# Attention with a threshold and two dense layers: k and q of a head pair turned by one crossbar transpose

## The chip, the cores and the metric

The kernel runs on one core of a Trainium2 chip. A core has five engines, each with its own instruction queue that is worked off in order: PE (TensorE, matrix products), DVE (VectorE), ACT (ScalarE), POOL (GpSimd) and SP (SyncE, which here only issues transfers). Sixteen DMA engines move data and can turn it on the way (the crossbar). The metric is device time of one execution in microseconds (us), lower is better.

## The reference

q, k and v have 8 batches, 8 heads, 576 rows and a head dimension of 64, in float32.

```
scores = matmul(q, k.T) / sqrt(64)
thresh = max(scores, axis=-1) - tau            # tau = 0.02
scores = where(scores >= thresh, scores, -1e9)
attn   = softmax(scores)
x      = matmul(attn, v)       # heads side by side: 4608 rows x 512
h      = x @ w_in              # 512 x 2048
out    = (h - tanh(h)) @ w_out # 2048 x 512
```

## The kernel before

**Pairs and slots.** Two heads of a batch make a pair; there are 32 (counted from 0). A pair has 1152 rows of q, nine tiles of 128: four of each head and one that the heads share. So there are 288 tiles, and the kernel is written out by hand as slots, one for each tile, 8 slots ahead for the scores: in slot s the scores of tile s + 8 are issued, the kink (threshold as a steep Prelu on ACT) of tile s + 5, the exponentials of tile s, and the product with v of tile s - 2. The two dense layers of an earlier batch lie between them, a few matmuls in a slot. Nothing is reordered: each engine gets its instructions in the order in which the slots issue them. The first scores of pair p come in slot 9p - 8, called `first` in the code.

**Why k and q are turned.** PE contracts over partitions, so k and q must lie with head dimension down the partitions. For accuracy each is also split into a high and a low half in float16 (`split`, lines 225 to 235, three POOL operations for each of k and q): 64 high and 64 low numbers fill 128 partitions. The split tile `khl` or `qhl` is 128 x 9 x 128, nine blocks of 128 x 128. Turning the blocks gives `kT` and `qT`, 128 x 1152. Scores need high and low parts crossed too, so POOL also copies kT with its halves exchanged to `kS` (`swap`, line 332, two copies).

**Two ways of turning.** For pairs 0 to 8 the blocks are turned on PE and copied from PSUM. From pair 9, the tenth, on (`k_by_dma`, `q_by_dma`), `turn` (line 311) issues a crossbar transpose of nine blocks from SP's queue, line 315, one for k and one for q. The tiles' threshold values z are turned the same way from pair 6 on: one transpose zT<-z of nine blocks for two tiles, issued on SP at line 454 as soon as the second tile's kink is issued; line 483 exponentiates zT on ACT five slots later. SP works all of these off in order, together with the stores of the output (line 620).

**When a step is issued.** For each pair from 8 on, a table gives the step and how many slots ahead of `first` it is issued: `LATER[0]` for even pairs, `LATER[1]` for odd ones, `FIRST_LATER` for pairs 8 and 9. In a step's name the first letter is the tensor, the second the step: 0, 1, 2 loads (issued on ACT's queue, in parts), s split on POOL, t turn, w swap on POOL. The table at lines 760 to 783 sets only the order in the queues; each step also waits for its data. An engine that waits holds all that is queued behind it.

**Buffers.** Raw k, q and v have two buffers each, split tiles two each, kT, qT and kS three each.

Of the kernel before, what the change touches and what calls it, by code (L numbers as in the profile page):

```python
# [11 lines left out]
FP16 = mybir.dt.float16  # L12
# [6 lines left out]
def kernel(  # L19
# [11 lines left out]
    nc = tc.nc  # L31
    P = 128

    B, H, S, D = q.shape
# [17 lines left out]
    TPP = 9  # L52
# [8 lines left out]
    W = 2 * S  # L61
# [51 lines left out]
    hl_pool = pool("hl", 2)  # L113
    qk_pool = pool("qk", 3)
# [29 lines left out]
    def load_part(p, t, part):  # L144


        b, h0 = p // HPAIR, 2 * (p % HPAIR)
        if part == 0:
            both = raw_pool.tile([P, AT_ONCE, 10, D], F32, name=f"{t}raw", tag=t)
            boths[t] = both  # L150
            for a in range(AT_ONCE):
                raws[p + a, t] = both[:, a, :, :]
        both = boths[t]
        rows = {"k": k, "q": q, "v": v}[t][b, h0 : h0 + 2 * AT_ONCE, :, :]
        heads = both.rearrange("p a (h c) d -> p (a h) (c d)", h=2)
        if t == "k":
            dst = both[:, :, 0:TPP, :].rearrange("p a c d -> p a (c d)")
            rows = rows.rearrange("(a h) s d -> a (h s) d", h=2).rearrange(
                "a (p c) d -> p a (c d)", c=TPP
            )  # L160
        elif t == "v":
            rows = rows.rearrange("h (p c) d -> p h (c d)", c=TPP)

            at, c0, c1 = V_PARTS[part]
            dst = heads[at : at + 64, :, c0 % 4 * D : (c1 - c0 + c0 % 4) * D]
            if c0 == 8:
                dst = heads[at : at + 64, :, 4 * D : 5 * D]
            rows = rows[:, :, c0 * D : c1 * D]
        elif part == 0:
            dst = heads[:, :, 0 : 4 * D]  # L170
            rows = rows[:, 0:512, :].rearrange("h (p c) d -> p h (c d)", c=4)
        else:
            dst = both[:, part - 1, 4, :]
            rows = rows[2 * part - 2 : 2 * part, 512:S, :].rearrange("h s d -> s h d")
        LOADER.dma_start(out=dst, in_=rows)
# [44 lines left out]
    for n in range(11):  # L220
        nc.tensor.matmul(out=pz, lhsT=zero[:, 0:P], rhs=zero, start=True, stop=True)

    hls = {}

    def split(p, t):
        x = raws.pop((p, t))[:, 0:9, :]
        hl = hl_pool.tile([P, TPP, 2, D], FP16, name=f"{t}hl", tag=t)
        nc.gpsimd.tensor_scalar(  # L228
            out=x, in0=x, scalar1=QKSC, scalar2=1.0, op0=ALU.mult, op1=ALU.mult
        )  # L230
        nc.gpsimd.tensor_copy(out=hl[:, :, 0, :], in_=x)
        nc.gpsimd.tensor_tensor(  # L232
            out=hl[:, :, 1, :], in0=x, in1=hl[:, :, 0, :], op=ALU.subtract
        )
        hls[p, t] = hl

    def split_first(t, part):
        cs = (slice(0, 5), slice(5, TPP))[part]
        r = raws[0, t][:, cs, :]
        if part == 0:  # L240
            hls[0, t] = hl_pool.tile([P, TPP, 2, D], FP16, name=f"{t}hl", tag=t)
        hl = hls[0, t][:, cs, :, :]
        if part == 0:
            nc.scalar.mul(out=hl[:, :, 0, :], in_=r, mul=QKSC)
            nc.vector.scalar_tensor_tensor(
                out=hl[:, :, 1, :], in0=r, scalar=QKSC, in1=hl[:, :, 0, :],
                op0=ALU.mult, op1=ALU.subtract,
            )
        else:
            nc.gpsimd.tensor_scalar(  # L250
                out=r, in0=r, scalar1=QKSC, scalar2=1.0, op0=ALU.mult, op1=ALU.mult
            )
            nc.gpsimd.tensor_copy(out=hl[:, :, 0, :], in_=r)
            nc.gpsimd.tensor_tensor(
                out=hl[:, :, 1, :], in0=r, in1=hl[:, :, 0, :], op=ALU.subtract
            )
# [13 lines left out]
    mats = {}  # L270


    def qk_tile(t):
        m = qk_pool.tile([P, W], FP16, name="kS" if t == "ks" else f"{t}T", tag=t)
        return m

    by_head = lambda ap: ap.rearrange("p (s h) -> p h s", h=2)
    in_heads = lambda ap: ap.rearrange("p (h s) -> p h s", h=2)
# [1 line left out]
    def turn_chunk(out, c, lhsT, mixed=True):  # L280
        rhs = ident_f16
        if c == 4 and mixed:
            out, rhs = in_heads(out), by_head(rhs)
        nc.tensor.matmul(
            out=out, lhsT=lhsT, rhs=rhs, is_transpose=True, start=True, stop=True
        )
# [17 lines left out]
    def q_by_dma(p):  # L304

        return p > DUAL

    def k_by_dma(p):
        return p > DUAL

    def turn(p, t):
        hl = hls.pop((p, t))
        if (q_by_dma if t == "q" else k_by_dma)(p):
            m = mats[p, t] = qk_tile(t)
            nc.sync.dma_start_transpose(
                out=m[:, 0:W].rearrange("p (c r) -> p c r", c=TPP),
                in_=hl.rearrange("p c a d -> p (c a d)"),
            )
            return
        ps = ps_big.tile([P, W], FP16, name=f"ps_{t}", tag="big")  # L320
        for c in range(TPP):
            turn_chunk(
                ps[:, c * P : (c + 1) * P], c, hl[:, c, :, :].rearrange("p a d -> p (a d)"),
                t == "q" or p < DUAL,
            )
        m = qk_tile(t)
        nc.vector.tensor_copy(out=m[:, 0:W], in_=ps)
        mats[p, t] = m
        if t == "k":
            swap(p)  # L330

    def swap(p):
        m = mats[p, "k"]
        sw = qk_tile("ks")
        for lo, hi in ((0, D), (D, 0)):
            o, i = sw[lo : lo + D, 0:W], m[hi : hi + D, 0:W]
            nc.gpsimd.tensor_copy(out=o, in_=i)  # L337
        mats[p, "ks"] = sw

    def turn_first(t, part):  # L340

        hl = hls[0, t[0]]
        c0, c1 = ((0, 5), (5, TPP))[part]
        pl, tag = (ps_y, "y") if t == "ks" else (ps_h, "h")
        ps = pl.tile([P, 5 * P], FP16, name=f"ps1_{t}", tag=tag)
        for c in range(c0, c1):
            o = ps[:, (c - c0) * P : (c - c0 + 1) * P]
            if t == "ks":
                for a in range(2):
                    turn_chunk(o[64 * a : 64 * a + 64, :], c, hl[:, c, 1 - a, :])  # L350
            else:
                turn_chunk(o, c, hl[:, c, :, :].rearrange("p a d -> p (a d)"))
        if part == 0:
            mats[0, t] = qk_tile(t)
        dst, n = mats[0, t][:, c0 * P : c1 * P], (c1 - c0) * P
        if part == 1 or t == "q":
            nc.scalar.copy(out=dst, in_=ps[:, 0:n])
        else:
            nc.vector.tensor_copy(out=dst, in_=ps[:, 0:n])
# [373 lines left out]
    def w_load(piece):  # L733
# [6 lines left out]
        else:  # L740
# [18 lines left out]

    LATER = {  # L760
        0: (
            ("kt", 11), ("qt", 7), ("k0", 18), ("q0", 17), ("v0", 13),
            ("q1", 14), ("v1", 10), ("ks", 12), ("qs", 8), ("vs", 4),
            ("kw", 6),
        ),
        1: (
            ("kt", 10), ("qt", 6), ("k0", 18), ("q0", 14), ("v0", 15),
            ("q1", 13), ("v1", 12), ("ks", 11), ("qs", 8), ("vs", 6),
            ("kw", 5),
        ),  # L770
    }
    FIRST_LATER = {
# [1 line left out]
            ("k0", 18), ("q0", 15), ("v0", 14), ("kt", 7), ("q1", 15),  # L774
            ("ks", 8), ("v1", 12), ("vs", 6), ("qs", 10), ("qt", 5),
            ("kw", 3),
        ),
        9: (
            ("kt", 10), ("qt", 6), ("k0", 18), ("q0", 14), ("v0", 15),
            ("q1", 13), ("v1", 12), ("ks", 11), ("qs", 8), ("vs", 6),  # L780
            ("kw", 5),
        ),
    }
    for p in range(DUAL, NPAIR):
        first = TPP * p - AHEAD
        at = lambda d, f: plan.setdefault(first - d, []).append(f)
        for what, d in FIRST_LATER.get(p) or LATER[p % 2]:
            t, w = what
            f = {
                "0": lambda p=p, t=t: load_part(p, t, 0),  # L790
                "1": lambda p=p, t=t: load_part(p, t, 1),
                "2": lambda p=p, t=t: load_part(p, t, 2),
                "s": lambda p=p, t=t: split_v(p) if t == "v" else split(p, t),
                "t": lambda p=p, t=t: turn(p, t),
                "w": lambda p=p, t=t: swap(p) if k_by_dma(p) else None,
            }[w]
            at(d, f)
    for p in range(1, DUAL):
        first = TPP * p - AHEAD
        for d, f in PREP[3 if p == 1 else 0 :]:  # L800
            d -= p == 1 and d == 3
            if p > HPAIR and d >= LDK - 2:
                d = ((16, 14, 12), (17, 15, 13))[1 - p % 2][LDK - d]
            elif d in (7, 8) and q_by_dma(p):
                d = ((9, 9) if d == 7 else (10, 10))[1 - p % 2]
            elif p in LEADS and d in (8, 7, 5, 4):
                d = LEADS[p][(8, 7, 5, 4).index(d)]
            elif d == 4:
                d = 4
            elif d == 5:  # L810
                d = k_lead(p)
            elif p in (2, 4):
                d = {8: 9, 7: 8}.get(d, d)
            plan.setdefault(first - d, []).append(lambda p=p, f=f: f(p))
        d = (6, 7)[1 - p % 2] if q_by_dma(p) else 3 - (p == 1 or p >= 5)
        d = LEADS[p][4] if p in LEADS else d
# [5 lines left out]
    for t in ("k", "q", "ks"):  # L822
        turn_first(t, 0)
# [28 lines left out]
    for s in range(-AHEAD, NTILE + LAG + 3):  # L852
        p, j = divmod(max(s, 0), TPP)
# [25 lines left out]
        if s == 0:  # L879
            nc.vector.tensor_tensor(  # L880
                out=fold, in0=ident_bf[:, 0:64], in1=ident_bf[:, 64:P], op=ALU.add
# [79 lines left out]
```

## Time and profile before

| | |
|---|---|
| median of 3 runs | 510.61 us (507.43 to 511.88) |
| the profiled execution | 504.09 us, its span 502.3 us |
| granted TensorE clock | 1.00 |
| busy share of the span | PE 96%, ACT 86%, DVE 80%, POOL 58% |
| DMA | 95.02 MB in 232157 packets |

The profile is of one execution. Busy time is the time in which an engine has at least one instruction in work; issuing a DMA doesn't count as busy. "DMA share" is the mean busy share of the 16 DMA engines, with transfers that overlap counted each. "To landing" is the time from the issue of a DMA to its completion. In a row such as `kT<-khl SPq DMA_TRANSPOSE x23`, kT is written and khl read, SPq is SP's queue, and 23 is the number of issues. In a row of waits, "POOL kS L337 <- DMA kT<-khl: 72.8, 23, 5.4", POOL's instruction of line 337 waited 72.8 us in total for that transfer, 23 times, 5.4 us at most.

### The profile page before, as it was taken

How to read it: one execution, taken by the hardware profiler on the slowest of the kernel's cores; microseconds unless marked ns; L12 is line 12 of the kernel's file. 1: busy time of each engine (PE TensorE's matmuls, PEld its weight loads, DVE VectorE, ACT ScalarE, POOL GpSimd, SP SyncE). 2: the span in 40 equal slices, each digit the busy share in tenths (PEclk: the TensorE clock that was granted, in tenths of full speed). 3: DMA queues.
4: the chain of work that ended last, by engine and by line, in shares of the span. 5: the costliest groups of instructions: out<-in, count | busy, mean ns of one | idle time of the engine just before them, and what ended most of it. 6: DMA issues, size and time to landing. Idle time of an engine off the chain costs nothing.

```text
span 502.3 us, 12201 instructions
## 1 busy us (share of the span) xinstructions
PE 482.5 (96%) x4292; PEld 270.5 (54%) x4354; DVE 400.8 (80%) x1151; ACT 431.9 (86%) x617; POOL 292.2 (58%) x390
## 2 busy tenths in 40 slices
PE   8999899989999999999999999999999999999997
PEld 4667566555555555555555555555555555444444
DVE  5899978988889898988898889889888887544430
ACT  5999999899999999999999999999989999434330
POOL 8999999897765675576575765658556600000000
PEclk9999999999999999999999999999999999999999
DMA  6852558999999999999999999999999965311003
GB/s 208 261 162 91 189 167 229 209 202 229 223 207 243 247 246 222 223 251 212 239 218 249 247 213 215 258 217 249 235 196 228 226 119 116 88 42 43 36 29 84
DMA packets 232157, 95.02 MB, mean 189 GB/s; under 512 B 202784, under 2 KB 221472, under 8 KB 232096
## 3 DMA queue, kind: packets, MB, share of 16 engines
q1 hardware_dynamic: 211152, 72.58, 75.4%
q10 hardware_dynamic: 20944, 21.67, 15.7%
q8 instruction: 34, 0.56, 0.5%
q14 instruction: 27, 0.22, 0.1%
HBM read 36.70 MB, written 9.44 MB: 92 GB/s over the span
## 4 chain that ended last, share of the span: by engine, by line
PE 74%; POOL 9%; ACT 5%; issue 4%; DVE 4%; DMA 2%; SPq 1%; ACTq 0%; POOLq 0%
PE psY L605 23%; PE psH L579 19%; PE psS L410 18%; PE psO L513 5%; PE psHt L579 3%; DMA kraw<-in_k_dram 2%; PE psS L401 2%; POOL kS L337 2%; ACT z L447 2%; DVE sc L420 1%; PE psO L524 1%; ACT pT L483 1%; ACT pT L475 1%; DVE g L598 1%; PE psO L506 1%
## 5 line engine op out<-in xcount | busy, mean ns | idle before, releaser
L420 DVE TENSOR_SCALAR_CACHE_REDUCE sc<-psS 128x576 f32<-128x576 f32 x288 | 213.5, 752 | 25.5 <-PE psS L410 12.4
L447 ACT ACTIVATE z<-sc,nb 128x576 bf16<-128x576 f32 x288 | 217.3, 773 | 8.6 <-DVE nb L432 6.1
L605 PE MATMUL psY<-w_out_sb,g 128*128 128x512 bf16 (+1 forms) x564 | 140.8, 373 | 1.6 <-issue 0.2
L483 ACT ACTIVATE pT<-zT 128x1152 f16<-128x1152 bf16 x117 | 135.4, 1157 | 4.8 <-DMA zT<-z 3.3
L579 PE MATMUL psH<-xT,w_in_sb 128*128 128x512 bf16 x448 | 118.8, 379 | 4.2 <-issue 1.7
L337 POOL COPY kS<-kT 64x1152 f16<-64x1152 f16 x62 | 70.9, 1144 | 76.6 <-DMA kT<-khl 72.8
L598 DVE SCALAR_TENSOR_TENSOR g<-th,psH 128x512 bf16<-128x512 f32 x128 | 87.6, 684 | 27.3 <-ACT th L592 26.3
L410 PE MATMUL psS<-kT,qT 128*128 128x512 f16 (+1 forms) x512 | 104.4, 285 | 3.2 <-DVE sc L420 1.9
L410 PE MATMUL psS<-kS,qT 128*128 128x512 f16 (+1 forms) x512 | 104.6, 286 | 0.0
L410 PEld LDWEIGHTS <-qT 128*128 128x128 f16 x1024 | 72.5, 97 | 57.8 <-issue 4.1
L592 ACT ACTIVATE th<-psH 128x512 f32<-128x512 f32 x128 | 74.9, 585 | 20.9 <-PE psH L579 20.9
L605 PEld LDWEIGHTS <-g 128*128 128x128 bf16 x592 | 51.1, 98 | 54.6 <-DVE g L598 0.4
L579 PEld LDWEIGHTS <-w_in_sb 128*128 128x128 bf16 x576 | 49.0, 98 | 55.9 <-issue 4.6
L513 PE MATMUL psO<-vb,pT 128*128 128x65 bf16 x1024 | 53.3, 194 | 0.0
L513 PEld LDWEIGHTS <-pT 128*128 128x128 f16 x1024 | 44.2, 98 | 10.0
L232 POOL TENSOR_TENSOR qhl<-qraw,qhl 128x576 f16<-128x576 f32 x31 | 39.7, 1282 | 2.6
L232 POOL TENSOR_TENSOR khl<-kraw,khl 128x576 f16<-128x576 f32 x31 | 39.7, 1281 | 2.6
L475 ACT ACTIVATE pT<-psZ 128x512 f16<-128x512 bf16 (+1 forms) x54 | 35.1, 653 | 2.5 <-PE psZ L466 2.2
L617 DVE COPY yo<-psY 128x512 f32<-128x512 f32 (+1 forms) x31 | 21.1, 679 | 13.0 <-PE psY L605 12.4
L539 DVE TENSOR_TENSOR osb<-psO,rc 128x256 bf16<-128x256 f32 x64 | 27.2, 425 | 2.2
L506 PE MATMUL psO<-vb,pT 128*128 128x130 bf16 x128 | 28.1, 220 | 0.1
L228 POOL TENSOR_SCALAR qraw<-qraw 128x576 f32<-128x576 f32 x31 | 20.9, 673 | 12.5 <-DMA qraw<-in_q_dram 12.5
(77 smaller groups left out, 453.0 us busy)
## 6 DMA issues: line engine op xcount, KB each, us to landing
out_dram<-yo SPq DMA_DIRECT2D x32, 256.0 KB, 3.6
kraw<-in_k_dram ACTq DMA_DIRECT2D x24, 288.0 KB, 4.5
qraw<-in_q_dram ACTq DMA_DIRECT2D x24, 256.0 KB, 4.3
wt<-in_moe_w_in_dram SPq DMA_DIRECT2D x8, 512.0 KB, 4.3
wt<-in_moe_w_out_dram SPq DMA_DIRECT2D x8, 512.0 KB, 4.3
vraw<-in_v_dram ACTq DMA_DIRECT2D x24, 160.0 KB, 4.1
vraw<-in_v_dram ACTq DMA_DIRECT2D x24, 128.0 KB, 3.9
vraw<-in_v_dram SPq DMA_DIRECT2D x8, 256.0 KB, 3.5
```

The source lines that it names most:

```text
L232: nc.gpsimd.tensor_tensor(out=hl[:, :, 1, :], in0=x, in1=hl[:, :, 0, :], op=ALU.subtract)
L337: nc.gpsimd.tensor_copy(out=o, in_=i)
L410: nc.tensor.matmul(out=ps[:, dst], lhsT=lhs, rhs=cols(p, kk, hh), start=(n == 0), stop=(n == 1),)
L420: nc.vector.tensor_scalar(out=sc, in0=ps[:, lo : lo + S], scalar1=SC, scalar2=None, op0=ALU.mult, op1=ALU.max, accum_out=mx[:, c : c + 1],)
L447: nc.scalar.activation(out=z, in_=sc, func=ACT.Prelu, bias=nb, scale=1.0, alpha=STEEP)
L475: nc.scalar.activation(out=pt[:, off * P : (off + n) * P], in_=ps[:, 0 : n * P], func=ACT.Exp)
L483: nc.scalar.activation(out=pt[:, 0 : n * P], in_=zts.pop(i)[:, 0:n, :], func=ACT.Exp)
L513: nc.tensor.matmul(out=po[:, t - 1 + ab, :], lhsT=pt[:, blk * P : (blk + 1) * P], rhs=vb[:, hh, c, :], start=False, stop=(n == 7), skip_gr ...
L579: nc.tensor.matmul(out=ps, lhsT=w_in_sb[:, c, n * P : (n + 1) * P], rhs=xs[m][:, c, :] if m < B else xR[:, c, :, :], start=(c == 0), stop= ...
L592: nc.scalar.activation(out=th, in_=ps, func=ACT.Tanh)
L598: nc.vector.scalar_tensor_tensor(out=gs[m][:, n, :], in0=th, scalar=-1.0, in1=ps, op0=ALU.mult, op1=ALU.add,)
L605: nc.tensor.matmul(out=ps, lhsT=gs[m][:, n, ms * P : (ms + 1) * P], rhs=w_out_sb[:, n, cols], start=(n == 0), stop=(n == DF_C - 1),)
```

## The change

From pair 9 on, k and q share one split tile `hl` (k in its first half, q in its second) and one turned tile `kqT`, and one transpose of 18 blocks turns both. The number of buffers is unchanged (two of hl, three of kqT), and so is the memory. The early pairs use halves of the same tiles and are turned on PE as before. The step "kq" replaces "kt" and "qt"; the table's other entries move; pair 9 has no entry of its own any more and takes that of odd pairs.

```diff
+    def hl_half(p, t):
+        if p not in hl_of:
+            hl_of[p] = hl_pool.tile([P, 2, TPP, 2, D], FP16, name="hl", tag="hl")
+        hls[p, t] = hl_of[p][:, int(t == "q"), :, :, :]
+        return hls[p, t]
...
     def split(p, t):
         x = raws.pop((p, t))[:, 0:9, :]
-        hl = hl_pool.tile([P, TPP, 2, D], FP16, name=f"{t}hl", tag=t)
+        hl = hl_half(p, t)
...
+    def qk_tile(p, t):
+        if t == "ks":
+            return qk_pool.tile([P, W], FP16, name="kS", tag=t)
+        if p not in both_of:
+            both_of[p] = qk_pool.tile([P, 2, W], FP16, name="kqT", tag="kq")
+        return both_of[p][:, int(t == "q"), :]
...
+    def turn_both(p):
+        for t in ("k", "q"):
+            mats[p, t] = qk_tile(p, t)
+            hls.pop((p, t))
+        nc.sync.dma_start_transpose(
+            out=both_of[p].rearrange("p t (c r) -> p (t c) r", c=TPP),
+            in_=hl_of[p].rearrange("p t c a d -> p (t c a d)"),
+        )
...
     LATER = {
         0: (
-            ("kt", 11), ("qt", 7), ("k0", 18), ("q0", 17), ("v0", 13),
-            ("q1", 14), ("v1", 10), ("ks", 12), ("qs", 8), ("vs", 4),
-            ("kw", 6),
+            ("k0", 21), ("q0", 20), ("q1", 18), ("v0", 13), ("v1", 11),
+            ("ks", 16), ("qs", 14), ("kq", 10), ("kw", 6), ("vs", 3),
         ),
         1: (
-            ("kt", 10), ("qt", 6), ("k0", 18), ("q0", 14), ("v0", 15),
-            ("q1", 13), ("v1", 12), ("ks", 11), ("qs", 8), ("vs", 6),
-            ("kw", 5),
+            ("k0", 19), ("q0", 17), ("q1", 16), ("v0", 14), ("v1", 13),
+            ("ks", 14), ("qs", 12), ("kq", 9), ("kw", 6), ("vs", 4),
         ),
     }
...
-        9: (
-            ("kt", 10), ("qt", 6), ("k0", 18), ("q0", 14), ("v0", 15),
-            ("q1", 13), ("v1", 12), ("ks", 11), ("qs", 8), ("vs", 6),
-            ("kw", 5),
-        ),
...
+                "q": lambda p=p: turn_both(p),
```

## The prediction

> **What bounds the kernel now.** I read the page's busy times, then the table of stretches, to see which engine has no room where the change works (pairs 9 to 31, counted from 0, about 70 to 405 us).
>
> ```profile
> PE 482.5 (96%) x4292; PEld 270.5 (54%) x4354; DVE 400.8 (80%) x1151; ACT 431.9 (86%) x617; POOL 292.2 (58%) x390
> ```
> ```profile
> 200.00:250.00 50.00, 49.37 (x440) 27.05 (x446) 43.87 (x130) 48.85 (x67) 32.43 (x42) 1.00 1.23 229
> 250.00:300.00 50.00, 49.53 (x436) 27.23 (x443) 44.17 (x132) 48.63 (x66) 34.09 (x44) 1.00 1.20 235
> 300.00:350.00 50.00, 49.37 (x444) 27.31 (x447) 44.67 (x133) 48.05 (x67) 32.53 (x42) 1.00 1.22 233
> ```
>
> Columns of a stretch: PE, PEld, DVE, ACT, POOL busy, granted clock, DMA share, GB/s. PE has 0.5 to 0.6 us of idle time in 50, at full clock; ACT has 1.2 to 2.0. PE sets the pace, so nothing that the change saves elsewhere is worth more than that idle time: some 5 us over the 320 us concerned. ACT, which feeds PE through the exponentials, could be pushed over the edge by little. The DMA share is above 1, so transfers already lie on top of each other.
>
> The pace itself I take from the chain of waits: the matmuls of L401 (the rows shared by two heads) come once in two pairs, and every second time in the same phase of the output layers' work.
>
> ```profile
> 166.61 1.11 PE psS L401 x16
> ...
> 219.49 1.11 PE psS L401 x16
> ...
> 272.37 1.11 PE psS L401 x16
> ```
>
> 272.37 - 166.61 = 105.8 us for eight pairs: 26.4 us for two, 1.47 us for a slot.
>
> Next the DMA issues, with the median time from issue to landing, and who waits for what:
>
> ```profile
> zT<-z SPq DMA_TRANSPOSE x117, 4.7
> ...
> kT<-khl SPq DMA_TRANSPOSE x23, 5.4
> qT<-qhl SPq DMA_TRANSPOSE x23, 3.8
> ```
> ```profile
> POOL kS L337 <- DMA kT<-khl: 72.8, 23, 5.4
> POOL qraw L228 <- DMA qraw<-in_q_dram: 12.5, 8, 3.8
> ...
> ACT pT L483 <- DMA zT<-z: 3.3, 7, 0.8
> ```
>
> POOL stands 3.2 us in each pair (72.8 / 23) for the turned k, with everything behind it in its queue. ACT waits for zT in only 7 of 117 cases: the z transposes land just in time.
>
> What nine blocks take alone is seen in a stretch with one transpose and no loads (40 slices of 0.1 us from 420 us):
>
> ```profile
> DMA  0000000000000059999999999999500000000000
> GB/s 0 0 0 0 0 0 0 0 0 0 0 0 0 8 105 205 212 220 218 195 236 200 197 218 223 187 177 246 93 13 0 0 0 0 0 0 0 0 0 0
> ```
>
> The packets flow for 1.5 us, at about 210 GB/s; the shortest landing of a z transpose is 3.2 us, so 1.7 us is issue and completion.
>
> **The change, part by part.** *Removed:* 23 transposes of nine blocks as instructions. SyncE is held 1.24 us or more by each (1.47 us at the median). PE and ACT don't wait for SyncE's issue time as such, so this saves at most 23 x 1.4 = 32 us of SyncE and nothing on PE. *Kept:* all blocks, splits, kS copies, loads and every instruction of PE, DVE and ACT.
>
> *The 18-block transpose* isn't in the trace. From below: a nine-block one plus 1.5 us of packets, alone 3.2 + 1.5 = 4.7 us. From above: SyncE's hold doubles too, and it lands like kT does: 5.4 + 1.5 + 1.3 = 8.2 us. Beside other traffic: like qT 3.8 + 1.5 = 5.3, like zT 4.7 + 1.5 = 6.2, like kT 5.4 + 1.5 = 6.9. I take 6.2, the largest group and in the middle.
>
> A rule would say otherwise. The Trainium skill ("Advanced Engine Details and Errata", X-Bar Transpose (TRN2)) expects 350 to 400 GB/s of a crossbar transpose; nine blocks of 32 KB would then flow in 0.8 us, and the estimate from that page for the big one like zT would be 5.5 us. The stretch above shows 210 GB/s for such a transpose with nothing beside it, so I stay with 1.5 us. Its rule to coalesce small transfers ("DMA: Bandwidth & Descriptors", Rules for kernel authors) speaks for the change: 1.7 us of fixed cost saved 23 times would be 39 us. But it holds only where the fixed costs stand one behind the other, and here the queue issues a transpose while earlier ones are in flight.
>
> *The moved steps.* In slots before the pair's first scores, k's transpose does not come sooner: 11 to 10 on even pairs, 10 to 9 on odd ones; q's comes three sooner (7 to 10, 6 to 9). Both splits come sooner (k 4 and 3 slots, q 6 and 4), k and q loads 1 to 4 (v loads move by one at most). Loads are issued in ACT's queue beside its activations; ACT's busy time doesn't grow. Their buffers were split off ten slots or more before, so they wait for nothing new. The casts of v move 1 to 2 slots later, with over ten slots until the first product with v; cover enough.
>
> *The new wait* is the heart of it: the one transpose needs q's split as well as k's, so k now waits for q's work on POOL. The built program's order on POOL over two pairs (e even, o odd) becomes: kS e, split k o, v e, split q o, (transpose o), split k of the next e, kS o, split q e, (transpose e), v o, kS e. Before, it was kS e, v e, split k o, (transpose o), split q o, v o, kS o, split k e, (transpose e), split q e, kS e: q's split lay inside the time of k's transfer. What each step takes on POOL:
>
> ```profile
> 213.80 2.33 POOL L337 COPY kS<-kT 64x1152 f16<-64x1152 f16 x2 [1.82 <-DMA kT<-khl]
> 216.22 0.67 POOL L228 TENSOR_SCALAR kraw<-kraw 128x576 f32<-128x576 f32 x1
> ...
> 218.96 0.67 POOL L228 TENSOR_SCALAR qraw<-qraw 128x576 f32<-128x576 f32 x1
> ...
> 220.44 1.28 POOL L232 TENSOR_TENSOR qhl<-qraw,qhl 128x576 f16<-128x576 f32 x1
> 224.67 2.33 POOL L337 COPY kS<-kT 64x1152 f16<-64x1152 f16 x2 [2.95 <-DMA kT<-khl]
> 227.06 0.62 POOL L261 CAST vb<-vraw 128x512 bf16<-128x512 f32 x1
> ...
> 228.47 0.67 POOL L228 TENSOR_SCALAR kraw<-kraw 128x576 f32<-128x576 f32 x1
> ```
>
> From start to next start: kS 2.4, a split of k 2.7 (216.22 to 218.96), of q 2.8, v 1.4. This is a closed loop: no step of it can start before the one ahead has ended. Before: 2 x 2.4 + 2 x 2.7 + 1.4 = 11.6 us, two landings of 5.4 and about 0.3 us from landings to copies: 22.7 us, against PE's 26.4. After: 2 x 2.4 + 2.7 + 2 x 2.8 + 1.4 = 14.5, plus 0.3, plus two landings of the big transpose: 14.8 + 2 L. The loop meets PE's pace at L = (26.4 - 14.8) / 2 = 5.8 us. With L = 6.2 it takes 27.2 us, 0.8 us more than PE needs, in each of the 11 double pairs: 9 us. Of this some 2 us is taken up once, since kS is finished ahead of its use: it ends at 216.13 for scores that start at 219.4, 3.3 us. Net 7 us.
>
> What waits behind it: on SyncE the z transposes, in order behind a transpose that waits for POOL. zT feeds ACT's exponential, and ACT has only 0.6 to 1.1 us to spare in two pairs, so a SyncE that is late becomes an ACT and then a PE that is late. This is how the loop's excess reaches the end, not a second cost added to it.
>
> *Sum.* The profiled execution took 504.1 us (span 502.3 and 1.8 around it): 504.1 + 7 = 511. The median of the runs shown is 510.6, 6.5 us above it, so I forecast 510.6 + 7, about 518 us.
>
> **The rivals.**
> *A, no difference.* L lands at 5.8 or under, the loop stays under PE's pace, and SyncE's saved time is worth nothing: 508 to 513. For it: qT lands in 3.8 us, and a SyncE that has stood waiting for q's split has few transposes in flight ahead of the big one.
> *B, faster.* The bunches of transposes are fewer and the loads are spread and earlier: POOL no longer waits for q's load (12.5 us before) and ACT not for zT. Price: the idle time of PE, 5 us, and what makes the runs without a profile 6.5 us longer than the profiled one, if late transfers make it; half of both gives 505. It decides if L is 5.3 or less, like qT, and z transposes land no later than before. Against it: the median zT shares the DMA engines with 1.5 us more in one piece.
> *C, ACT late at once.* The z transpose just behind the big one lands 1.5 us later, while ACT has about 0.4 us to spare in a pair: up to 1.1 us in each of 22 pairs, 24 us; as zT lands late only in some pairs, half of it, 12 us: 523. It needs no loop. Against it: q's transpose no longer stands in front of another zT.
> *D, the transpose lands like kT.* L = 6.9: 28.6 - 26.4 = 2.2 us in 11 double pairs, 24 - 2 = 22: 533.
>
> **How the numbers follow.** Forecast 0.35 (L 5.9 to 6.5: 512 to 524), A 0.25, B 0.15, C 0.15, D 0.10. Under 1% (505 to 516 around 510.6) can hardly be told from no change. Faster by over 1%: B, 0.15. Within: A and the low third of the forecast less a little, 0.33. Slower: 0.52. The range reaches from half of B, 505, to D's near edge, 533. Of both signs, the forecast's own range is 512 to 524.
>
> **What would show it.** The row kqT<-hl among the DMA issues (x23): its median is L; 5.8 us divides the cases. POOL's wait of kS for it: at 6.2 us, (6.2 - 1.4) + (6.2 - 2.7) = 8.3 us in two pairs, 91 us in all, against 72.8. SyncE's waits of the big transpose for POOL's split of q (12.5 us in 8 before, for L232) should grow in nearly all of 23. ACT's wait for zT rises from 3.3 us, and PE's busy share between 200 and 350 us falls below 98%. The forecast is wrong if POOL's two-pair rhythm stays 26.4 us with SyncE not waiting for q's split, or if SyncE takes q's split with no one late behind it.

## The result and the profile after

The changed kernel takes 528.33 us (median of 4 runs, 526.14 to 530.46), the kernel before beside it 509.81: a ratio of 1.0405 with a 95% interval of 1.0355 to 1.0455. It is slower by 18.5 us in the medians and some 20 by the ratio; 7 were forecast. A ratio with its interval counts only runs within 1.5% of the fastest of their kernel, since some runs fall in a slower state, while a median counts all runs, so the two need not agree. The profiled execution took 527.49 us, its span 525.7, 23.4 more than before.

The busy times and the stretches, with the columns as before:

```profile
PE 491.6 (94%) x4292; PEld 273.6 (52%) x4354; DVE 400.8 (76%) x1151; ACT 433.2 (82%) x617; POOL 290.7 (55%) x390
```
```profile
200.00:250.00 50.00, 45.41 (x385) 24.49 (x392) 37.99 (x111) 43.78 (x60) 29.80 (x40) 0.97 1.15 214
250.00:300.00 50.00, 48.31 (x429) 26.30 (x434) 42.62 (x129) 44.66 (x61) 29.45 (x37) 1.00 1.16 215
300.00:350.00 50.00, 45.87 (x399) 24.98 (x407) 39.94 (x117) 46.55 (x64) 31.84 (x42) 0.97 1.10 213
```

The same numbers of instructions run on every engine but in more time. PE stood idle for 1.7 us of these 150 before and for 10.4 now; DVE, ACT and POOL are less busy in a stretch too. None of them has become the bound. Something outside them is late.

The DMA issues (median time to landing), and the groups of waits of all engines, the three longest:

```profile
zT<-z SPq DMA_TRANSPOSE x117, 4.6
...
kqT<-hl SPq DMA_TRANSPOSE x23, 6.4
```
```profile
POOL kS L356 <- DMA kqT<-hl: 100.0, 20, 8.9
DVE g L617 <- ACT th L611: 61.8, 66, 4.6
ACT pT L502 <- DMA zT<-z: 23.4, 15, 4.3
```

The big transpose lands in 6.4 us. The median z transpose is no slower than before (4.6 against 4.7). Yet ACT now waits for zT 23.4 us in 15 places, where it waited 3.3 in 7. The rise of 20.1 us is most of the span's 23.4. The chain of waits from 150 to 400 us, by line, begins before with `PE psS L410 28.6%; PE psH L579 24.9%; PE psY L605 24.9%`; now a transfer leads it:

```profile
by line: DMA zT<-z 20.9%; DMA kqT<-hl 11.3%; PE psY L624 10.1%; PE psS L429 9.7%; PE psH L598 8.3%; issue 6.1%; POOL hl L238 3.2%; ACTq L175 2.8%; ACT pT L502 2.7%; PE psO L532 2.2%; POOL hl L237 2.1%; ACT z L466 2.1%; POOL kS L356 2.0%; DV
```

One place shows how. SP's own timeline (start, duration, line), ACT's, and the chain over the same stretch:

```profile
203.80 4.81 SPq L325 DMA_TRANSPOSE kqT<-hl  x1
208.71 5.96 SPq L473 DMA_TRANSPOSE zT<-z  x3
```
```profile
204.91 0.77 ACT L466 ACTIVATE z<-sc,nb 128x576 bf16<-128x576 f32 x1
...
214.50 1.16 ACT L502 ACTIVATE pT<-zT 128x1152 f16<-128x1152 bf16 x1 [2.48 <-DMA zT<-z]
```
```profile
202.49 1.28 POOL hl L238
203.77 0.57 POOL vb L266
...
205.03 3.58 SPq L325
208.61 0.04 issue
...
208.71 5.71 DMA zT<-z
...
214.50 0.36 ACT pT L502
```

The split of q that the big transpose needs ends at 203.77 (202.49 + 1.28). SP's record of the issue starts at 203.80 and lasts 4.81 us, until 208.61: this time, in which SP can do nothing else, is called the hold here. (The chain lays its first 1.23 us to POOL's cast of v, which ended in it but which the transpose doesn't read.) z is complete at 205.68 (204.91 + 0.77), so its transpose starts 3.0 us after its data. It lands at 214.42, and ACT has stood still for 2.48 us. Before, the transposes of k and q of this pair, the seventeenth, had two of z between them:

```profile
193.01 1.29 SPq L315 DMA_TRANSPOSE kT<-khl  x1
194.39 4.09 SPq L454 DMA_TRANSPOSE zT<-z  x2
198.59 1.32 SPq L315 DMA_TRANSPOSE qT<-qhl  x1
```

The tile's rows give the issue's time for all 23, first of the changed kernel, then of the one before (ns, min/median/max):

```profile
L325 SPq DMA_TRANSPOSE kqT<-hl x23: 2616/3220/5272, 106.0 to 419.8; - x23
```
```profile
L315 SPq DMA_TRANSPOSE kT<-khl x23: 1287/1558/2966, 103.8 to 393.6; - x23
...
L315 SPq DMA_TRANSPOSE qT<-qhl x23: 1297/1377/2320, 109.1 to 399.3; - x23
```

Nine blocks hold SP for 1.29 us at least and 1.56 at the median as kT, 1.30 and 1.38 as qT: the hold goes with the blocks. One issue in place of two saves SP nothing (the holds sum to 77.5 us now and to 74.8 before), and what was held in two pieces with z transposes between them is now held in one.

I sorted the z transposes of pairs 10 to 29 by their place in the cycle of two pairs, nine of them to a cycle. Before, each is issued 0.0 to 1.2 us after its z is ready (medians by place). Now the one right behind the big transpose of even pairs is issued 2.95 us late, the one behind that of odd pairs 2.46; all others 0.0 to 1.8. ACT's waits stand in the same two places, 17.2 and 3.7 us, 20.9 of the 21.4 counted there.

### The profile page after: what moved, and what is told of

It is laid out like the page before. It is cut to its first block, busy times and chain, and to the rows that moved or that the text cites. A ratio compares the mean times of both kernels' runs of the same rounds, so it can differ in the third digit from the quotient of the medians.

```text
span 525.7 us, 12079 instructions
## 1 busy us (share of the span) xinstructions
PE 491.6 (94%) x4292; PEld 273.6 (52%) x4354; DVE 400.8 (76%) x1151; ACT 433.2 (82%) x617; POOL 290.7 (55%) x390
## 4 chain that ended last, share of the span: by engine, by line
PE 38%; DMA 20%; POOL 19%; issue 8%; ACT 7%; DVE 5%; ACTq 2%; SPq 1%; POOLq 0%
PE psY L624 14%; DMA zT<-z 10%; PE psH L598 10%; DMA kqT<-hl 8%; PE psS L429 7%; POOL hl L238 5%; POOL kS L356 4%; POOL hl L237 3%; PE psHt L598 3%; ACT pT L502 2%; ACT z L466 2%; PE psO L532 2%; POOL qraw L234 2%; ACTq L175 2%; DVE g L617 2%
## 5 line engine op out<-in xcount | busy, mean ns | idle before, releaser
L439 DVE TENSOR_SCALAR_CACHE_REDUCE sc<-psS 128x576 f32<-128x576 f32 x288 | 213.4, 751 | 24.8 <-PE psS L429 12.3
L502 ACT ACTIVATE pT<-zT 128x1152 f16<-128x1152 bf16 x117 | 135.1, 1155 | 23.5 <-DMA zT<-z 23.4
L624 PE MATMUL psY<-w_out_sb,g 128*128 128x512 bf16 (+1 forms) x564 | 143.0, 378 | 1.6 <-issue 0.2
L356 POOL COPY kS<-kqT 64x1152 f16<-64x1152 f16 x62 | 70.8, 1142 | 118.7 <-DMA kqT<-hl 100.0
L598 PE MATMUL psH<-xT,w_in_sb 128*128 128x512 bf16 x448 | 120.1, 382 | 8.2 <-DVE g L617 4.9
L429 PE MATMUL psS<-kqT 128*128 128x512 f16 (+1 forms) x512 | 105.5, 288 | 7.6 <-DVE sc L439 6.4
L429 PEld LDWEIGHTS <-kqT 128*128 128x128 f16 x1024 | 73.5, 98 | 63.9 <-issue 11.1
L429 PE MATMUL psS<-kS,kqT 128*128 128x512 f16 (+1 forms) x512 | 105.8, 289 | 0.0
L611 ACT ACTIVATE th<-psH 128x512 f32<-128x512 f32 x128 | 74.6, 583 | 20.9 <-PE psH L598 20.9
L598 PEld LDWEIGHTS <-w_in_sb 128*128 128x128 bf16 x576 | 49.7, 98 | 61.1 <-issue 10.2
L238 POOL TENSOR_TENSOR hl<-qraw,hl 128x576 f16<-128x576 f32 x31 | 39.7, 1280 | 2.6
L238 POOL TENSOR_TENSOR hl<-kraw,hl 128x576 f16<-128x576 f32 x31 | 39.7, 1280 | 2.6
L636 DVE COPY yo<-psY 128x512 f32<-128x512 f32 (+1 forms) x31 | 21.1, 679 | 13.0 <-PE psY L624 12.4
L558 DVE TENSOR_TENSOR osb<-psO,rc 128x256 bf16<-128x256 f32 x64 | 27.2, 424 | 2.2
L485 PE MATMUL psZ<-ident_bf,z 128*128 128x128 bf16 x243 | 22.5, 220 | 2.3 <-ACT pT L494 1.4
```

What stands on the lines that cost most here:

```text
L238: nc.gpsimd.tensor_tensor(out=hl[:, :, 1, :], in0=x, in1=hl[:, :, 0, :], op=ALU.subtract)
L429: nc.tensor.matmul(out=ps[:, dst], lhsT=lhs, rhs=cols(p, kk, hh), start=(n == 0), stop=(n == 1),)
L439: nc.vector.tensor_scalar(out=sc, in0=ps[:, lo : lo + S], scalar1=SC, scalar2=None, op0=ALU.mult, op1=ALU.max, accum_out=mx[:, c : c + 1],)
L502: nc.scalar.activation(out=pt[:, 0 : n * P], in_=zts.pop(i)[:, 0:n, :], func=ACT.Exp)
L598: nc.tensor.matmul(out=ps, lhsT=w_in_sb[:, c, n * P : (n + 1) * P], rhs=xs[m][:, c, :] if m < B else xR[:, c, :, :], start=(c == 0), stop= ...
L611: nc.scalar.activation(out=th, in_=ps, func=ACT.Tanh)
```

## The experiments

**First question: POOL's loop, as predicted, or the hold on SP?** If the loop of splits, transposes and copies sets the pace, its length must show in the time, 11 times over. The first of four kernels has everything of the changed kernel, table and loads too, but k and q with tiles of their own and two transposes one behind the other:

```diff
-            ("ks", 16), ("qs", 14), ("kq", 10), ("kw", 6), ("vs", 3),
+            ("ks", 16), ("qs", 14), ("kt", 10), ("qt", 10), ("kw", 6), ("vs", 3),
...
-            ("ks", 14), ("qs", 12), ("kq", 9), ("kw", 6), ("vs", 4),
+            ("ks", 14), ("qs", 12), ("kt", 9), ("qt", 9), ("kw", 6), ("vs", 4),
```

> The changed table of slots, but with two transposes of nine blocks, k's and right behind it q's, in the slot of the 18-block one; k and q have tiles of their own as in the kernel before. SyncE is still held for 18 blocks and z transposes still stand behind them and behind q's split; only kS no longer waits for q. Loop theory (kS, the next split of q, the transpose and kS again form a circle on POOL and the crossbar that is longer than PE's two pairs of 26.4 us): the circle is cut, 508 to 514 us. Hold theory (SyncE is held 2.6 us or more by 18 blocks, so the z transpose behind lands too late for ACT, circle or not): 522 to 530 us. Loads theory (the moved loads meet the transposes): 522 to 530 us as well.

Measured: 522.88 us, ratio 1.0323 (1.0233 to 1.0413). The interval overlaps that of the change. ACT waits 24.8 us for zT, so most of the loss is there without a double-size instruction; whether the one instruction costs the rest (the medians differ by 5.45 us) is not shown.

The next changes the order on POOL, so that the copy kS of the odd pair no longer stands before the split that the next transpose needs; the loop is cut:

```diff
-            ("ks", 14), ("qs", 12), ("kq", 9), ("kw", 6), ("vs", 4),
+            ("ks", 14), ("qs", 12), ("kq", 9), ("kw", 4), ("vs", 4),
```

> The changed kernel with one number altered: on odd pairs the swap stands 4 slots ahead instead of 6, which puts the split of the next pair's q ahead of it on POOL; the 18-block transpose, its slots and all loads stay. Loop theory: the circle is cut (about 22.6 us where PE needs 26.4), 509 to 515 us. Hold theory: 523 to 530 us, for the transpose holds SyncE as before. Loads theory: 523 to 530 us.

Two more take a cast of v (1.4 us) out of the loop's path, or put the other one in: `("vs", 3)` of even pairs to 2, and `("vs", 4)` of odd pairs to 6.

> The changed kernel with the cast of v on even pairs 2 slots ahead instead of 3: it then stands behind the split of q on POOL, outside the circle, which gets 1.4 us shorter in two pairs. Loop theory: 11 x 1.4 = 15 us less than the changed kernel, 512 to 517 us. Hold theory: within 2 us of the changed kernel, 526 to 530 us.

> The changed kernel with the cast of v on odd pairs 6 slots ahead instead of 4: it then stands between the swap and the next split of q, inside the circle, which gets 1.4 us longer in two pairs. Loop theory: 11 x 1.4 = 15 us more than the changed kernel, 540 to 546 us. Hold theory: within 3 us of the changed kernel, 526 to 531 us.

Measured: 527.18 us, 1.0388 (1.0335 to 1.044) with the loop cut; 525.04, 1.0354 (1.029 to 1.0418) with 1.4 us less in it; 529.97, 1.043 (1.0365 to 1.0494) with 1.4 us more. The loop's theory asked for 11 x 1.4 = 15 us between each of the last two and the change; they lie 3 below and 2 above. The loop is not what limits. With the loop cut, ACT's wait is as long as ever:

```profile
POOL kS L356 <- DMA kqT<-hl: 97.5, 15, 11.6
ACT pT L502 <- DMA zT<-z: 28.3, 18, 4.4
```

**Second question: the transposes in a row, or the loads?** The table also moves loads, which share the DMA engines. The first kernel moves only these, on the kernel before:

```diff
-            ("kt", 11), ("qt", 7), ("k0", 18), ("q0", 17), ("v0", 13),
-            ("q1", 14), ("v1", 10), ("ks", 12), ("qs", 8), ("vs", 4),
+            ("kt", 11), ("qt", 7), ("k0", 21), ("q0", 20), ("v0", 13),
+            ("q1", 18), ("v1", 11), ("ks", 12), ("qs", 8), ("vs", 4),
...
-            ("kt", 10), ("qt", 6), ("k0", 18), ("q0", 14), ("v0", 15),
-            ("q1", 13), ("v1", 12), ("ks", 11), ("qs", 8), ("vs", 6),
+            ("kt", 10), ("qt", 6), ("k0", 19), ("q0", 17), ("v0", 14),
+            ("q1", 16), ("v1", 13), ("ks", 11), ("qs", 8), ("vs", 6),
```

> The kernel before with the changed kernel's slots for the loads alone (k 21 and 19, q 20, 18 and 17, 16, v 11, 14, 13); splits, swaps and the two transposes of nine blocks stay. Loads theory (the moved loads run beside the transposes and make the z transposes late): 518 to 526 us. Hold theory (18 blocks in a row on SyncE make the z transpose behind them late): no difference to before, 505 to 512 us.

Measured: 529.49 us, 1.0396 (1.0318 to 1.0475). With not one transpose changed, the loads alone cost as much as the whole change. This was a surprise. The waits and the issues of that kernel:

```profile
POOL kS L337 <- DMA kT<-khl: 98.6, 20, 8.3
ACT pT L483 <- DMA zT<-z: 31.7, 22, 2.8
```
```profile
zT<-z SPq DMA_TRANSPOSE x117, 5.2
```

ACT's wait for zT again, but elsewhere: the z transposes as a whole land 0.5 us later than before, and the waits fall on four other places of the cycle (9.7, 6.2, 4.8 and 7.9 us), none on the two that are late in the changed kernel. Two of the four (9.7 and 7.9 us) are issued in time, 0.4 and 0.0 us after their z at the median as in the kernel before, but land in 7.3 and 7.9 us instead of 4.9 and 4.8. And k's transposes hold SP for 2.32 us at the median instead of 1.56, without a block more.

The same question from the other side: the change with its loads and splits, but with k's and q's transposes three slots apart again (`("kt", 10), ("qt", 7)` on even and `("kt", 9), ("qt", 6)` on odd pairs in place of "kq", with tiles of their own).

> As e1_two_nines (the changed table, two transposes of nine blocks), but q's transpose three slots behind k's, as in the kernel before, so that one z transpose stands between them on SyncE. Hold theory: the z transposes are in time again, 507 to 514 us, against 522.9 of e1_two_nines. Loads and splits theory (what else the table moved costs the time): 519 to 526 us.

Measured: 519.84 us, 1.0243 (1.0173 to 1.0312), with 12.8 us of waits for zT. Against the changed kernel that gains 8.5 us (528.33 - 519.84), and the lateness behind the row is gone (1.36 and 0.47 us in the two places); the remaining 10 us are there without any row. But the kernel with the two transposes in a row differs from this one in q's slot alone, and there the gain is 3.0 us (522.88 - 519.84), with intervals that overlap, though ACT's wait for zT falls from 24.8 to 12.8 us.

Two kernels were to give z a slot more on its way, by issuing the kink one slot sooner (`MASK = 5` to 6), on the change and on the kernel before.

> The changed kernel with the kink one slot sooner (MASK 6 for 5), so each z transpose has 1.47 us more until its exponential. Hold theory: ACT's wait for zT falls from 23 us to under 8 and the time to 512 to 518 us. Theory that PE waits for kS or q itself and ACT's waits only follow: no gain, 526 us or more. ACT may wait more for DVE's nb; the same edit of the kernel before, run beside it, shows that.

> The kernel before with the kink one slot sooner (MASK 6 for 5), as the control of e6_mask6. Its z transposes are late in only 7 of 117 cases (3.3 us), so hold theory gives 503 to 510 us; if the earlier kink makes ACT wait for DVE, 510 to 520 us.

Measured: 551.78 us, 1.0698 (1.0599 to 1.0797), and 534.01, 1.051 (1.0451 to 1.0568). The control loses 24 us by itself: ACT then waits 38.9 us for the thresholds that the kink needs (nothing for zT). So this pair can't test the remedy. It hints that late zT is not all of the loss: the change stays above its control (its two faster runs, 541.4 and 546.0, by 7 and 12 us), although ACT waits only 3.9 us for zT in its profile, which is of a run of 557.59 us.

**Third question: do the loads cost by lying close together?** In the changed table k's and q's loads fall into fewer slots. Two kernels take the loads of k and q of even pairs alone (k0 21, q0 20, q1 18) and of odd pairs alone (19, 17, 16) on the kernel before. A third spreads the loads of the changed kernel, a fourth those of the kernel with the transposes apart:

```diff
-            ("k0", 21), ("q0", 20), ("q1", 18), ("v0", 13), ("v1", 11),
+            ("k0", 21), ("q0", 19), ("q1", 18), ("v0", 13), ("v1", 11),
...
-            ("k0", 19), ("q0", 17), ("q1", 16), ("v0", 14), ("v1", 13),
+            ("k0", 19), ("q0", 17), ("q1", 16), ("v0", 8), ("v1", 7),
```

(with the odd pairs' v cast one slot later, `("vs", 3)`).

> The kernel before with the k and q loads of even pairs alone in the changed kernel's slots (21, 20, 18). They then stand right behind the odd pair's v and q loads: 1120 KB of loads issued in five slots. Bunch theory (it is loads standing close together in time, among the transposes, that make the z transposes late): 525 to 535 us. Sooner theory (each load that starts sooner costs, wherever it stands): about half of what all of them cost, 515 to 522 us.

> The kernel before with the k and q loads of odd pairs alone in the changed kernel's slots (19, 17, 16). They then stand farther from the odd pair's v loads: no more than 448 KB in two slots, as before. Bunch theory: no loss, 503 to 511 us. Sooner theory: about half of what all of them cost, 515 to 522 us.

> The changed kernel with its 18-block transposes and splits as they are, but the loads spread: v of odd pairs 8 and 7 slots ahead instead of 14 and 13 (its cast 3 instead of 4), q of even pairs 19 instead of 20, so that no longer 832 KB are issued in four slots. Bunch theory: most of the loss goes, 508 to 517 us, and what is left is the 18-block transpose's own. Hold theory (18 blocks on SyncE by themselves): 523 to 530 us. Sooner theory: 520 to 528 us, for the k and q loads stay as soon.

> As e7_apart (the changed table with two transposes of nine blocks, q's three slots behind k's) with the loads spread as in e11_spread. Bunch theory: 504 to 511 us, with no 18 blocks in a row. Its difference to e11_spread is the price of the one big transpose: 3 to 8 us by what e1_two_nines and e7_apart differed, none if the big transpose costs nothing.

Measured: even pairs 520.31 us, 1.0226 (1.0166 to 1.0287); odd pairs 517.85, 1.0144 (1.006 to 1.0228; three runs lie at 515.8 to 517.9, two at 526.1 and 529.4); spread 525.72, 1.033 (1.0256 to 1.0405); spread and apart 515.0, 1.0129 (1.0073 to 1.0184). The bunch as a cause fell: each half of the loads costs something, and spreading them doesn't help the changed kernel beyond its interval. It helps the one with the transposes apart a little. But the row of transposes shows again: 525.72 - 515.0 = 10.7 us between the last two, which differ in the row, its shared tiles and its wait for both splits.

**Fourth question: what does the row cost by itself, and is late zT all of it?** Two kernels leave k's and q's transposes and the loads of the kernel before and add work that the reference doesn't ask for: a further transpose of k's nine blocks to a spare tile, in one kernel right behind k's, in the other two slots later. Bytes and issues are the same in both.

```diff
+    def extra(p):
+        nc.sync.dma_start_transpose(
+            out=spare, in_=hl_last[p].rearrange("p c a d -> p (c a d)")
+        )
...
+            if what == "kt" and p > DUAL:
+                at(d, lambda p=p: extra(p))
```

(`at(d - 2, ...)` in the second).

> The kernel before with one more transpose of nine blocks (khl once more, into a spare tile that nobody reads) right behind each of the 23 k transposes, so that SyncE issues 18 blocks in a row; loads, splits and all else in their slots of before. Hold theory: the z transpose behind has to wait some 1.3 to 3 us more and had 1.4 us at the median, 520 to 530 us. Bytes theory (only the nine blocks more of traffic count, wherever they stand): the same time as e16_alone within 3 us.

> As e15_row, but the extra transpose two slots later, with a z transpose between it and k's: the same blocks and bytes, never more than nine in a row except by chance. Hold theory: cheaper than e15_row by 5 us or more, 511 to 520 us. Bytes theory: the same as e15_row within 3 us.

Measured: in a row 553.82 us, 1.0834 (1.0748 to 1.092); alone 537.56, 1.0546 (1.0465 to 1.0628). SP's timeline of the first and of the second:

```profile
197.04 1.54 SPq L317 DMA_TRANSPOSE kT<-khl  x1
198.69 2.08 SPq L337 DMA_TRANSPOSE spare<-khl  x1
200.88 4.30 SPq L463 DMA_TRANSPOSE zT<-z  x2
```
```profile
203.40 2.05 SPq L317 DMA_TRANSPOSE kT<-khl  x1
205.55 1.32 SPq L463 DMA_TRANSPOSE zT<-z  x1
206.92 2.73 SPq L337 DMA_TRANSPOSE spare<-khl  x1
209.74 1.41 SPq L463 DMA_TRANSPOSE zT<-z  x1
```

In the first, z's transposes stand behind 18 blocks; in the second one goes in between. That order alone is worth 553.82 - 537.56 = 16 us, and it is seen in ACT's wait, in the first and in the second:

```profile
ACT pT L492 <- DMA zT<-z: 50.2, 26, 4.8
```
```profile
ACT pT L492 <- DMA zT<-z: 35.8, 34, 3.1
```

With no load moved and no tile shared, a row of 18 blocks makes the z transposes behind it late, as in the changed kernel. Both kernels lost more than was expected of them, by over 15 us. And 23 x 9 blocks more, well placed, cost 28 us (537.56 - 509.99), so there was little room left on SP's queue and the crossbar before the change.

The other two kernels of this set give ACT the room: the exponentials of pairs 9 to 26 are issued one slot later, with the dense layers' pattern shifted by as much, on the change and on the kernel before.

```diff
-        at = i - SOONER[min(i // TPP, 6)]
+        at = i - SOONER[min(i // TPP, 6)] + (9 <= i // TPP < 27)
```

> The changed kernel with the exponentials and the products with v of pairs 9 to 26 one slot later, so that each of their z transposes has 1.47 us more to land; scores, kinks, transposes and loads stay in their slots. Late-z theory (the whole loss is ACT waiting for the z transpose behind the big one): its waits fall from 23 us to about 10 and the time by 10 to 15 us, to 513 to 518 us. Theory that the lateness follows from PE or DVE: within 3 us of the changed kernel.

> The same edit of the kernel before, as the control. Its z transposes are late in only 7 of 117 cases: 505 to 511 us; over 515 us if later exponentials cost time by themselves, and then e13_slack has to be read against this.

Measured: 1.026 (1.017 to 1.0349) for the change with the slot (median 527.66, but the four runs lie at 523.0, 524.0, 531.3 and 532.6) and 0.9988 (0.9938 to 1.0038) for the control. So the slot is free where zT is in time, and takes some 1.4% off the changed kernel by the lower two runs; the upper two are as slow as the change without it. Its chain still has the transposes in front:

```profile
by line: DMA kqT<-hl 24.9%; DMA zT<-z 13.7%; issue 9.0%; ACT z L466 6.3%; POOL hl L238 5.3%; PE psH L598 4.7%; PE psS L429 4.6%; PE psY L624 3.8%; POOL hl L237 3.5%; POOL kS L356 3.4%; ACT pT L502 3.3%; ACT th L611 2.7%; ACTq L175 2.5%; POO
```

ACT waits 9.4 us for zT, and 4.4 us before it may write z, whose buffer a late z transpose still reads; behind these comes the big transpose with its kS copy.

**Last question: is POOL's loop the next limit, once ACT has the slot?** The slot's kernel with the loop cut (odd `("kw", 4)`, even `("vs", 2)`), and, to see the loads alone with the slot, the moved loads on the kernel before with it.

> As e13_slack, with the circle on POOL cut as well: the swap of odd pairs 4 slots ahead instead of 6 (behind the split of the next q) and the cast of v of even pairs 2 instead of 3. If the circle is the second limit behind the late z transposes: 511 to 518 us against 527.7 of e13_slack (523 to 533). If it is not, within 4 us of e13_slack.

> As e5_loads_only (the kernel before with the loads alone moved, 529.5 us), with the exponentials and the products with v of pairs 9 to 26 one slot later. If the moved loads cost their time through z transposes late for ACT (31.7 us of waits there): 509 to 516 us, waits for zT under 10 us. If they cost it in another way: 520 us or more.

Measured: 521.42 us, 1.0275 (1.015 to 1.04), and 521.34, 1.0277 (1.0205 to 1.0349). Cutting the loop gains little here too: its runs lie at 519.8, 519.9, 522.9 and 533.9 against 523.0, 524.0 and up without the cut, and the intervals overlap. What is left stands in ACT's two kinds of wait for z transposes, in the first and in the second:

```profile
ACT z L466 <- DMA zT<-z: 9.4, 7, 2.1
ACT pT L502 <- DMA zT<-z: 8.6, 7, 1.8
```
```profile
ACT z L447 <- DMA zT<-z: 9.5, 5, 3.7
...
ACT pT L483 <- DMA zT<-z: 5.3, 7, 1.2
```

With the slot, the price of the loads falls from 19.9 us (529.49 - 509.64) to 12.4 (521.34 - 508.97), not to nothing. No kernel beat the one before; the control with the slot equals it.

**All of them on one scale.** The span of each profiled execution above the 502.3 us of before, beside ACT's waits for z transposes in it (for zT, and for the buffer of z):

| kernel | span above before | ACT's waits for z transposes |
|---|---|---|
| the change | 23.4 | 23.4 |
| two transposes in a row | 18.5 | 24.8 |
| loop cut | 23.2 | 28.3 |
| loop shorter / longer | 23.6 / 22.5 | 28.6 / 27.3 |
| loads alone, all / of even pairs | 26.0 / 15.9 | 31.7 / 12.0 |
| transposes apart | 11.8 | 12.8 |
| spread / spread and apart | 22.1 / 12.2 | 28.8 / 10.2 |
| extra transpose in a row / alone | 47.9 / 32.7 | 50.2 / 35.8 |
| slot / slot and loop cut | 19.9 / 15.7 | 13.8 / 18.0 |
| slot and loads alone | 16.5 | 14.8 |
| slot, on the kernel before | 8.0 | 1.1 |
| kernel before | 0 | 3.3 |

The two follow each other within 7 us. That is a parallel and not yet a cause: the slot took 9.6 us off the changed kernel's waits and 3.5 off its span. All the differences are taken from one execution of the kernel before, 504.09 us long where its median is 509.81, and would be some 5 us smaller against a typical one. (The odd pairs' loads are left out: that profiled execution took 529.35 us against a median of 517.85. The kernels with the kink sooner are too, as their time goes elsewhere.) Whatever was changed, ACT lost time where a z transpose came late, and the kernel lost about as much.

## Why the prediction was right or wrong

**Right: the direction, the place of the bound, and the big transpose's duration.** The direction was luck as far as the forecast's own reason goes: it was to come from the loop, and the loop doesn't set the time. 6.2 us was forecast for L, 6.4 measured (4.6 to 9.3). The 6.4 is the middle of two groups that the working didn't tell apart, about 7.8 us on even pairs and 4.7 on odd ones; their sum, 12.5, is near the 12.4 of 2 L. POOL's wait for it is 100 us against 91 forecast. That PE has 98.8% of a stretch and ACT a microsecond to spare, so that anything late shows, held too. 528 lies in the range of 505 to 533.

**Wrong: the term of the sum.** "With L = 6.2 it takes 27.2 us, 0.8 us more than PE needs, in each of the 11 double pairs: 9 us", less 2, was the only cost. The loop does stretch, but cutting it, shortening it and lengthening it by 1.4 us moved the time by 1 to 3 us. And in the changed kernel's own waits PE stands for POOL's copy only once:

```profile
PE psS L420 <- POOL kS L356: 0.4, 1, 0.4
```

POOL's 100 us of waiting for the turned k are its own affair. At fault is an earlier step, "PE and ACT don't wait for SyncE's issue time as such". They do, at one remove. The hold of an 18-block issue, 3.2 us at the median, makes the z transpose behind it 2.5 to 3 us late, in two places where zT had landed 1.5 and 1.8 us before its use (medians of before).

**Rival C had the mechanism, at the wrong price.** I priced "the z transpose just behind the big one" at 1.5 us late, up to 24 us, and halved it on the ground that few zT were late before. It was 2.5 to 3 us late in the median, and ACT's waits behind the big transposes sum to 20.9 us: the whole of the price, not half. Its "against", that q's transpose no longer stands before another zT, is true: those z transposes come in time now. But they had been in time enough before, and time gained where there is slack pays nothing.

**"This is how the loop's excess reaches the end, not a second cost added to it"** was wrong for the same reason: the lateness behind the big transpose needs no loop.

**SyncE's wait for POOL's split of q** was to grow from 12.5 us in 8 cases to nearly all of 23. The view of SP's waits gives 38.0 us in 18 cases now (7.9 of it for the cast of v, which isn't read) and 39.1 in 32 before, for k and q together. But it counts up to POOL's last signal before the issue ends, needed or not. The starts of the records tell more: each of these issues starts within 0.1 us of the later of two ends, that of its split and that of SP's instruction before it. By that measure SP hardly stood for a split before, 0.1 us once, so the 12.5 us that I read were none; now it does in 12 of 23 cases, 9.4 us in all, ten of them on odd pairs, while 17.2 us of ACT's waits stand behind even ones. Nor does it set the time: with the loop 1.4 us shorter no issue waits for its split, with the loop 1.4 us longer 18 do, for 19.1 us, and the two kernels take 525.04 and 529.97 us.

**The saved issues.** The sum gave "at most 32 us of SyncE". It was nothing: 23 holds of 3.2 us at the median against 23 of 1.6 plus 23 of 1.4. I had put "SyncE's hold doubles too" among the bounds, but only as part of L, not as a delay of what is queued behind. The Trainium skill would have told the direction ("DMA: Bandwidth & Descriptors", the table of issue costs under Why a DMA increments its semaphore by 16 and not by 1): for "previous generations", without naming this chip, it has a transpose within SBUF pushed tile by tile, and from that its issue would grow with its size. The measured 1.3 and 2.6 us at the shortest agree with that. The rule to coalesce, which I let speak for the change, is for small transfers and names 64 KB; nine blocks are 288 KB.

**Loads "wait for nothing new"** was right for their buffers and blind to what they meet. Moved alone, they cost 20 us, with ACT waiting at four other z transposes. In the changed kernel those four are not late, so the two prices can't be added.

**What stays open.** How the 20 us divide between the row and the loads. The row was worth 16 us with the loads of before and extra blocks, 10.7 with the spread loads and 8.5 with the changed ones, the last two with the one instruction and its waits in it; as q's slot alone, 3.0. What remains without it (10 us) goes with the table of loads and splits; each move of a transfer shifts which z transposes collide. Splits were not moved alone. Nor is it shown why a further slot for ACT buys only a part: z's buffers were seen to be waited for then, but a kernel with more of them was not tried.

## What to carry to other kernels

A queue that issues just-in-time transfers is a resource with latency: before two issues become one, compare the time that the larger one holds the queue with the slack of whoever waits for the next transfer, one place of the cycle after the other, and not with sums of busy time. A long total wait (POOL's 100 us) names no bound; change it by a known amount and see whether the time follows. And where transfers are placed slot by slot around each other, moving loads by a few slots is a change of its own, to be tried by itself.

## What the runs showed of the hardware

**The clock fell in gaps that were short.** In the changed kernel's profile the clock is at half in four stretches of 3.41 us, from 160.0, 218.1, 303.4 and 361.4 us; before, in none until the very end. PE's timeline around the second:

```profile
215.72 0.23 PE L525 MATMUL psO<-vb,pT 128*128 128x130 bf16 x1 [1.22 <-ACT pT L502]
...
216.29 0.41 PE L429 MATMUL psS<-kS,kqT 128*128 128x512 f16 x2
218.27 0.64 PE L429 MATMUL psS<-kqT 128*128 128x512 f16 x2 [1.57 <-DVE sc L439]
218.72 0.67 PE L429 MATMUL psS<-kS,kqT 128*128 128x512 f16 x2
...
221.70 0.41 PE L429 MATMUL psS<-kS,kqT 128*128 128x512 f16 x2
```

Two score matmuls take 0.41 us before, 0.64 and 0.67 after two gaps of 1.2 and 1.6 us close together, and 0.41 again at 221.7. Of the 3.4 us before each of the four stretches PE was idle for 2.1 to 2.4 us, never for 3.4 at once. In each of the 20 traces of this case the clock changes only on a grid of 3.41 us. Cut by it (from 15 us on), the 24 windows with 1.95 us of idle PE or more were all followed by half speed, and none with less than 1.85 was unless half speed already ran; in between it went both ways, three and three. So the idle time in a fixed window counted, and not the longest gap: with two transposes in a row PE was idle for 2.44 us of the 3.41 that end at 130.6, but across two windows, and the clock stayed full. (The ends of matmuls are modelled in the trace.) The Trainium skill ("TensorE: Matmul & The Clock Gate", HAM oscillation — how this bites in real kernels) gives the rule as no idle gaps over about 3.4 us; here gaps of 1.4 to 2.3 us were enough, and the measurement decides. Half speed for 4 x 3.41 us is worth at most 6.8 us, and it can be most of what PE's busy time grew by (482.5 to 491.6). It comes on top of the late zT and isn't needed for the loss: two transposes in a row lose 18.5 us of span at full clock, the loads alone 26.0.

**An issue's hold varies.** 2.6 us is the shortest for 18 blocks, 5.3 the longest. The big transposes of even pairs, with five or six loads in flight beside each, hold SP for 3.8 us at the median and land in about 7.8; those of odd pairs, with none to two, hold it for 2.7 and land in about 4.7. So loads can reach the z transposes through SP's hold too, and not only through the DMA engines.
